# Soft-capped attention and a soft mixture of experts on one core: half tiles of the output started four products earlier, two evictions and a copy cut in two, and 14 more unused products

## The chip, the core and the metric

The kernel runs on one core of a Trainium2 chip. The core has five engines that run side by side, each with its own queue of instructions in order: TensorE (PE, matrix products, with loads of weights shown as PEld), VectorE (DVE), ScalarE (ACT), GpSimd (POOL) and SyncE (SP, which here only issues transfers). Products go to PSUM, a memory of eight banks, and from there ACT or DVE "evict" them, that is, copy them to SBUF, the large memory on the chip. Transfers between SBUF and HBM run on 16 DMA engines. The metric is the device time of one execution in microseconds.

## The reference

Sizes: 8 batches, 12 heads, 448 tokens, 64 columns a head; then 3584 rows of 768 columns, 8 experts with 4 slots each, hidden width 1024.

```python
scores = cap * tanh((q @ k.T) * scale / cap)
attn = exp(scores - max); attn = attn / (attn.sum(-1) + 1e-9)
x = (attn @ v)                       # as (3584, 768)
logits = x @ phi                     # (3584, 32)
d = softmax(logits, over the rows)
slot_input = d.T @ x                 # (32, 768)
for e in range(8):                   # 4 slots of each expert
    slot_out[e] = relu(slot_input[e] @ w1[e]) @ w2[e]
c = softmax(logits, over the slots)
out = c @ slot_out                   # (3584, 768), fp32
```

## The kernel before, in words

The program orders every engine's instructions by hand (`manual_schedule`); the framework adds the semaphores that the data and the banks need.

**Attention** fills the first 237 us. The 336 pairs of a key tile and two heads are worked off in 56 chunks of six (`CH`); chunk by chunk ACT takes the tanh and the exponential, DVE takes a part of the exponentials by a polynomial, and PE makes scores, the products with v, transposes and logits. What else is done in a chunk hangs in a table by chunk and slot (`at`, `run`). The table `FILL` (L805) puts unused products there: `fill(n)` (L661) issues n products of 57 columns whose result nobody reads. The row (7, 'a') of `FILL` applies to seven chunks: 7, 14, 21 and so on to 49.

**The weights** w1 and a part of w2 come to SBUF in this time; the rest of w2 is spilled to HBM as bf16 and fetched back by SP into `w2t` (L1057 to L1060) from 223 us on, when attention's buffers come free.

**The tail** starts with the last logits and slot sums (up to L1047). Then:

- `layer1` (L1074) multiplies the slots with w1, four experts at a time, and `relu` evicts; `h_transp` (L1091) turns the result. The order on PE is 72 products of layer 1, 8 of `h_transp(0)`, 48 of layer 1, 16 of layer 2, 8 of `h_transp(1)`, the rest of layer 2.
- `layer2` (L1105) multiplies with w2. Each call issues four products of 384 columns, for four experts, into one bank. The 64 products of half 0 (the first 384 output columns; L1161 to L1167) add up in `so_ps[0]`, the 64 of half 1 (L1170 on) in `so_ps[1]`.
- Between, L1168 copies the sum of half 0 to `so[0]` on ACT.
- While half 1 runs, 12 *half tiles* of the output are made from `so[0]` (L1173 to L1176). `half_tile` (L1142) issues one product of 384 columns into a bank of its own, has ACT or DVE scale it by `winv` into SBUF, and has SP store it (`store`, L1133). They come in pairs, one evicted by ACT and one by DVE.
- L1177 copies the sum of half 1 on DVE. The same 12 tiles then get their half 1, stored two at a time (L1190), and the last 16 tiles are made whole (L1192 to L1206).

PE, ACT, DVE and SP each work in the order in which these lines issue. A store waits for the eviction of what it writes.

Of the kernel before, what the change touches and what calls it, by code (L numbers as in the profile page):

```python
# [18 lines left out]
P = 128  # L19
# [18 lines left out]
def kernel(  # L38
# [18 lines left out]
    HD = D // 2  # L57
# [12 lines left out]
    pe, dve, act, pool, sp = nc.tensor, nc.vector, nc.scalar, nc.gpsimd, nc.sync  # L70
# [17 lines left out]
    winv = consts.tile([P, B // 2, NT], F32, name="winv")  # L88
# [655 lines left out]
    def et_tile(bb, c):  # L744
        return (ETl if bb == B // 2 - 1 else ET4[:, bb])[:, c, :, :].rearrange("p a q -> p (a q)")
# [50 lines left out]
    def at(j, slot, f, *a):  # L796
        if j < 0:
            j, slot = 0, "b"
        aux.setdefault((j, slot), []).append((f, a))
# [2 lines left out]

        busy(n, psV.tile([P, parts * P], F32, name="junk", tag="pv"))

    FILL = ((7, 'a', fill, 25), (6, 'c', spare, 7), (5, 'a', fill, 8),)  # L805
    PER = 2 * NQB * NT // CH
    assert PER == 7 and NQB == 3

# [15 lines left out]
    for b in range(B):  # L824
# [11 lines left out]
        if b == 0:  # L836
            at(j + 1, "d", spare, 14)
            at(j + 2, "d", spare, 5)
        for k, slot, f, n in FILL:
            if (b or k > 2) and j + k < NCH - 1:  # L840
# [110 lines left out]
    def bank(shape, dt=F32, name="bank"):  # L951
        n = turns.pop(0)
        if not turns:
            turns.extend((3, 2, 6, 0, 1))
        return big.tile(shape, dt, name=name, tag=f"b{n}")
# [147 lines left out]
    so_ps = []  # L1103

    def layer2(n0, half):  # L1105
        for n in range(n0, n0 + 4):
            i, ft, gg = blocks[n]
            pe.matmul(so_ps[half][32 * gg:32 * gg + NS, :],  # L1108
                      hpad[:, 4 * i + gg, ft, :],
                      w2_half(n, half),  # L1110
                      start=(n0 == 0), stop=(n0 == len(blocks) - 4))
# [6 lines left out]
    so = [t[:, 0:HD] for t in room]  # L1118
# [14 lines left out]
    def store(n, h0, h1, src, tokens=1):  # L1133
        bb, c = divmod(n, NT)
        width = (h1 - h0) * HD
        sp.dma_start(out=bass.AP(tensor=out.tensor,
                                 offset=(2 * bb * S + c) * D + h0 * HD,
                                 ap=[[NT * D, P], [1, tokens * D]] if width == D else
                                 [[NT * D, P], [D, tokens], [1, width]]),
                     in_=src)  # L1140

    def half_tile(n, half, home, eng):  # L1142

        bb, c = divmod(n, NT)
        if c == 0:
            obs[bb, half] = wts.tile([P, NT, HD], F32, name="obh", tag="w1", bufs=E)
        ob = obs[bb, half][:, c, :]
        pe.matmul(home, et_tile(bb, c), so[half], start=True, stop=True)  # L1148
        if eng == "dve":
            dve.tensor_scalar_mul(ob, home, winv[:, bb, c:c + 1])  # L1150
        else:
            act.mul(ob, home, winv[:, bb, c:c + 1])
        k = waiting.pop(half, n)
        if half and n + 1 < NH and c < NT - 1 and k == n:
            waiting[half] = n
            return
        store(k, half, half + 1, obs[bb, half][:, c - (n - k):c + 1, :], n - k + 1)

    NH = 12
    n2 = len(blocks)  # L1160
    for n0 in range(0, n2, 4):  # L1161
# [3 lines left out]
            for b in (B - 2, B - 1):  # L1165
                e_recips(b)
        layer2(n0, 0)  # L1167
    act.copy(so[0], so_ps[0])  # L1168
    done = 0
    for n0 in range(0, n2, 4):  # L1170
        layer2(n0, 1)

        if n0 % 8 == 4 and n0 > 4 and done < NH:  # L1173
            for eng in ("act", "dve"):
                half_tile(done, 0, bank([P, HD], name="op0"), eng)
                done += 1  # L1176
    dve.tensor_copy(so[1], so_ps[1])  # L1177
    mid.close()
# [3 lines left out]
    for n in range(B // 2 * NT):  # L1182
        bb, c = divmod(n, NT)
        if n == NH + 3:
            e_transp(B - 1)
        if n == NH + 5:
            e_transp(B - 2)
        op = fin.tile([P, 2, 512], F32, name="op", tag="op")
        if n < NH:
            half_tile(n, 1, op[:, 0, 0:HD], "act" if n % 2 else "dve")  # L1190
            continue
        for half in range(2):  # L1192
            pe.matmul(op[:, half, 0:HD], et_tile(bb, c), so[half],  # L1193
                      start=True, stop=True)

        if n == NH or c == 0 or full:
            ob, n1 = wts.tile([P, 2, 2, HD], F32, name="ob", tag="w1", bufs=E), n
        dst = ob[:, n - n1, :, :]
        if n % 2:
            dve.tensor_scalar_mul(dst, op[:, :, 0:HD], winv[:, bb, c:c + 1])  # L1200
        else:
            act.mul(dst, op[:, :, 0:HD], winv[:, bb, c:c + 1])  # L1202
        full = n > n1 or c == NT - 1
        if full:
            store(n1, 0, 2, ob[:, 0:n - n1 + 1, :, :].rearrange("p t a d -> p (t a d)"),
                  n - n1 + 1)  # L1206
# [35 lines left out]
```

## Time and profile before

| | us |
|---|---|
| median of three runs | 283.37 |
| the three runs | 282.81, 283.37, 283.69 |
| the profiled execution | 283.45 |
| its span in the trace | 281.7 |

The page of a profile gives each engine's busy time as a share of the span, then the span in 40 slices, the DMA queues, and the chain of work that ended last: from the last instruction back, at each step to whatever released it. "issue" in that chain is time in which an engine waited for nothing that the profile shows. A group's row gives line, engine, operation, the tile that is written and those that are read, the shapes, the number of instructions, their busy time, the mean of one in ns, and the idle time ahead of them with what ended it. A timeline's row gives start, length, engine, line and what was done; "x28" are 28 instructions that follow each other. The start of a product in the timeline is when it enters PE, and several overlap.

### The profile page before, as it was taken

What the parts mean: (1) busy time and instruction counts of PE and PEld (TensorE: products, weight loads), DVE (VectorE), ACT (ScalarE), POOL (GpSimd) and SP (SyncE); (2) the same over time, 40 slices, a digit from 0 to 9 for tenths busy, and PEclk for the clock granted to TensorE, in tenths of its full rate; (3) what the DMA queues carried; (4) which work ended last, traced back from release to release, by engine and by line L of the source; (5) the groups of instructions that cost most, each with busy time, mean ns of one, the idle gap of its engine ahead of it and who ended that gap; (6) DMA issues with size and microseconds to landing.
All of it is one profiled execution on the core that took longest, in us unless ns stands there. A gap on an engine that the chain in (4) does not pass through costs nothing.

```text
span 281.7 us, 10449 instructions
## 1 busy us (share of the span) xinstructions
PE 246.5 (88%) x4563; PEld 167.0 (59%) x4563; DVE 239.5 (85%) x474; ACT 249.1 (88%) x198; POOL 140.9 (50%) x198
## 2 busy tenths in 40 slices
PE   8897889998998999889998999899988999997720
PEld 7555556756665766566656675667565777642410
DVE  3479999999999999999999999999999996447840
ACT  3999999999999999999999999999999997236730
POOL 7885548662957285727673768285744120200000
PEclk9999999999999999999999999999999999999995
DMA  7999999999999999999999999999999589959997
GB/s 245 245 190 203 218 211 227 228 223 217 206 218 225 219 231 226 225 216 213 221 226 215 207 220 230 217 219 214 231 217 220 128 260 317 408 201 391 413 424 303
DMA packets 58332, 68.08 MB, mean 242 GB/s; under 512 B 4144, under 2 KB 54448, under 8 KB 58288
## 3 DMA queue, kind: packets, MB, share of 16 engines
q0 software_dynamic: 42448, 35.31, 79.7%
q1 hardware_dynamic: 15552, 31.89, 32.4%
q8 instruction: 35, 0.57, 0.7%
q10 hardware_dynamic: 288, 0.23, 0.3%
q14 instruction: 9, 0.07, 0.1%
HBM read 91.72 MB, written 19.27 MB: 394 GB/s over the span
## 4 chain that ended last, share of the span: by engine, by line
ACT 38%; PE 31%; DVE 20%; issue 5%; POOL 1%; DVEq 0%; ACTq 0%
ACT ex L374 16%; ACT ex L366 14%; PE pv L635 8%; ACT ex L362 7%; PE sc L349 4%; DVE xq L645 2%; DVE xp L615 2%; PE so_ps L1108 2%; PE hp L1080 2%; DVE xp L613 2%; DVE ex L616 2%; ACT ob L1202 2%; PE op L1193 1%; DVE xf L612 1%; PE op L1148 1%
## 5 line engine op out<-in xcount | busy, mean ns | idle before, releaser
L366 ACT ACTIVATE ex<-sc 128x1344 f16<-128x1344 f32 (+1 forms) x91 | 118.5, 1405 | 1.5 <-PE sc L349 1.5
L374 ACT ACTIVATE ex<-ex 128x1344 bf16<-128x1344 f16 (+5 forms) x58 | 110.2, 1911 | 0.1
L635 PE MATMUL pv<-vbd,ex 128*128 128x130 bf16 (+1 forms) x1610 | 95.0, 212 | 9.5 <-POOL vbd L289 3.9
L635 PEld LDWEIGHTS <-ex 128*128 128x128 bf16 (+1 forms) x1680 | 75.6, 101 | 38.1 <-issue 6.2
L289 POOL CAST vbd<-vraw 64x896 bf16<-64x896 f32 x46 | 47.3, 1027 | 60.2 <-PE pv L635 42.5
L349 PE MATMUL sc<-qT,kT 64*64 64x448 bf16 x672 | 66.4, 359 | 5.6 <-ACT ex L366 4.1
L349 PEld LDWEIGHTS <-kT 64*64 64x64 bf16 x672 | 22.4, 105 | 14.4 <-ACT ex L366 6.3
L645 DVE TENSOR_TENSOR xq<-pv,rec 128x448 bf16<-128x448 f32 x46 | 28.7, 625 | 1.6
L362 ACT ACTIVATE ex<-sc 128x2688 f16<-128x2688 f32 x11 | 28.1, 2552 | 0.1
L615 DVE TENSOR_TENSOR xp<-xp,xf 128x1344 f16<-128x1344 f16 (+2 forms) x34 | 27.5, 808 | 0.5
L616 DVE TENSOR_TENSOR ex<-ex,xp 128x1344 uint16<-128x1344 uint16 (+2 forms) x34 | 26.9, 791 | 0.2
L613 DVE TENSOR_TENSOR xp<-xf 128x1344 f16<-128x1344 uint16 (+2 forms) x34 | 26.9, 790 | 0.2
L116 POOL DMA_DIRECT2D w1b<-in_moe_w_dram x32 | 25.8, 808 | 0.0
L281 DVE COPY kT<-kps 128x896 bf16<-128x896 bf16 x23 | 14.2, 616 | 4.9 <-PE kps L276 2.8
L610 DVE TENSOR_SCALAR ex<-ex 128x1344 uint16<-128x1344 f16 (+2 forms) x34 | 17.0, 501 | 1.2 <-ACT ex L362 0.7
L614 DVE TENSOR_SCALAR xp<-xp 128x1344 f16<-128x1344 f16 (+2 forms) x34 | 17.0, 500 | 0.6
L612 DVE TENSOR_SCALAR xf<-ex 128x1344 uint16<-128x1344 uint16 (+2 forms) x34 | 17.2, 507 | 0.3
L185 POOL DMA_DIRECT2D qb<-in_q_dram x22 | 16.3, 739 | 1.5 <-PE qps L279 0.9
L297 POOL MEMSET vbd<- 64x1 bf16 x22 | 3.0, 138 | 27.7 <-PE pv L635 27.4
L617 DVE TENSOR_SCALAR ex<-ex 128x1344 uint16<-128x1344 uint16 (+2 forms) x34 | 16.5, 484 | 0.2
L185 POOL DMA_DIRECT2D kb<-in_k_dram x22 | 16.5, 748 | 0.0
L120 POOL DMA_DIRECT2D w2d<-in_moe_w_dram x21 | 16.1, 789 | 0.0
(124 smaller groups left out, 320.6 us busy)
## 6 DMA issues: line engine op xcount, KB each, us to landing
w1b<-in_moe_w_dram POOLq DMA_DIRECT2D x32, 384.0 KB, 9.6
vraw<-in_v_dram SPq DMA_DIRECT2D x44, 224.0 KB, 6.3
w2d<-in_moe_w_dram POOLq DMA_DIRECT2D x21, 384.0 KB, 9.7
w2t<-w2d SPq DMA_DIRECT2D x21, 384.0 KB, 6.5
out_dram<-ob SPq DMA_DIRECT2D x7, 768.0 KB, 6.8
qb<-in_q_dram POOLq DMA_DIRECT2D x22, 224.0 KB, 8.1
kb<-in_k_dram POOLq DMA_DIRECT2D x22, 224.0 KB, 7.7
w2b<-in_moe_w_dram POOLq DMA_DIRECT2D x11, 384.0 KB, 8.9
```

What stands on the lines that cost most here:

```text
L116: pool.dma_start(out=w1b[e][:, js, fs], in_=w1r[:, e, js, fs])
L185: pool.dma_start(out=t, in_=quad_ap(nm, Q))
L289: pool.tensor_copy(vbds[Q % 2][r, :, :, c0:c0 + DH], raw[r])
L349: ins = pe.matmul(sc[cs, u, 0:S], qkT["k", Q][r, c, cs], qkT["q", Q][r, :, cs], start=True, stop=True).ins
L362: apart["t", i - 1] = apart["t", i] = act.activation(exs[j].bitcast(F16), own["board"][:, :, 0:S], ACT.Tanh, scale=qk_scale / cap).ins
L366: ins = act.activation(exs[j][:, half * CS + u0:half * CS + u1, :].bitcast(F16), (own[0] if i == u0 == 0 else sc)[:, u0:u1, 0:S], ACT.Tanh ...
L374: act.activation(exs[j][:, u0:u1, :], exs[j][:, u0:u1, :].bitcast(F16), ACT.Exp, scale=cap)
L613: lambda: dve.tensor_tensor(p, s, s.bitcast(F16), op=ALU.mult),
L615: lambda: dve.tensor_tensor(p, p, s, op=ALU.mult),
L616: lambda: dve.tensor_tensor(y, y, p, op=ALU.add),
L635: pe.matmul(out_, exs[j][r, u, q0:q0 + (HP if tail else P)], v_, start=(c == 0 and g == gs[0] < NF), stop=(c == NT - 1), skip_group_check= ...
L645: dve.tensor_tensor(xq[Q][:, h, s0:s1, :], pv[:, 0:s1 - s0, 0:DH], rec.to_broadcast([P, s1 - s0, DH]), op=ALU.mult)
```

## The change

Four edits. The fills of row (7, 'a') have 27 products in place of 25, in seven chunks: 14 products in all. The half tiles of half 0 come after the layer-2 calls n0 = 8, 16, ..., 48 of half 1, and not after 12, 20, ..., 52: each pair stands one call, four products, earlier, and three calls follow the last pair in place of two. The first pair (n0 = 8) is evicted in two column halves, by ACT and then by DVE in the order of issue; the later pairs as before. The copy of the half-0 sum is cut likewise, 192 columns on ACT and 192 on DVE.

```diff
-    FILL = ((7, 'a', fill, 25), (6, 'c', spare, 7), (5, 'a', fill, 8),)
+    FILL = ((7, 'a', fill, 27), (6, 'c', spare, 7), (5, 'a', fill, 8),)
...
         pe.matmul(home, et_tile(bb, c), so[half], start=True, stop=True)
-        if eng == "dve":
-            dve.tensor_scalar_mul(ob, home, winv[:, bb, c:c + 1])
-        else:
-            act.mul(ob, home, winv[:, bb, c:c + 1])
+        cut = {"act": HD, "dve": 0, "both": HD // 2}[eng]
+        if cut:
+            act.mul(ob[:, 0:cut], home[:, 0:cut], winv[:, bb, c:c + 1])
+        if cut < HD:
+            dve.tensor_scalar_mul(ob[:, cut:HD], home[:, cut:HD], winv[:, bb, c:c + 1])
...
-    act.copy(so[0], so_ps[0])
+    act.copy(so[0][:, 0:HD // 2], so_ps[0][:, 0:HD // 2])
+    dve.tensor_copy(so[0][:, HD // 2:HD], so_ps[0][:, HD // 2:HD])
     done = 0
     for n0 in range(0, n2, 4):
         layer2(n0, 1)
 
-        if n0 % 8 == 4 and n0 > 4 and done < NH:
+        if n0 % 8 == 0 and n0 > 0 and done < NH:
             for eng in ("act", "dve"):
-                half_tile(done, 0, bank([P, HD], name="op0"), eng)
+                half_tile(done, 0, bank([P, HD], name="op0"), eng if n0 > 8 else "both")
                 done += 1
```

## The prediction

> **What bounds the kernel now.** I read the page first, then the stretches of the last 35 us, the chain of waits through them, the timeline for single instructions, and last the queues. The attention part, up to about 237 us, is shared out over PE, ACT and DVE; all of the change but the fills acts behind it. From the page:
>
> ```profile
> span 281.7 us, 10449 instructions
> PE 246.5 (88%) x4563; PEld 167.0 (59%) x4563; DVE 239.5 (85%) x474; ACT 249.1 (88%) x198; POOL 140.9 (50%) x198
> q8 instruction: 35, 0.57, 0.7%
> ```
>
> By stretch of the tail (stretch, its length, busy time of PE, PEld, DVE, ACT and POOL, clock, DMA share, GB/s):
>
> ```profile
> 246.00:248.00 2.00, 2.00 (x63) 1.32 (x55) 0.90 (x4) 0.47 (x1) 0.00 (x0) 1.00 1.05 414
> 250.00:251.00 1.00, 0.91 (x16) 0.44 (x17) 0.00 (x0) 0.00 (x0) 0.00 (x0) 1.00 0.08 31
> 254.00:258.00 4.00, 2.88 (x32) 0.86 (x27) 3.06 (x6) 2.15 (x4) 0.00 (x0) 1.00 1.05 393
> 259.00:279.00 20.00, 8.71 (x46) 4.08 (x45) 10.32 (x14) 9.06 (x12) 0.00 (x0) 0.90 1.03 417
> ```
>
> From 254 us to the end the transfers are full (share 1.03 to 1.05): the output's 11.0 MB (3584 x 768 fp32) is being written. From 250 to 251 next to nothing moves (0.08): the last weights are in, and no output is ready. So the end moves with the moment from which stores flow without a gap. What sets that moment stands in the chain of waits (start, length, what):
>
> ```profile
> 240.69 4.05 PE hp L1080 x72
> 244.74 0.29 PE hps L1097 x8
> 245.03 1.42 PE hp L1080 x48
> 246.46 0.65 PE so_ps L1108 x16
> 247.11 0.29 PE hps L1097 x8
> 247.40 2.22 PE so_ps L1108 x49
> 249.62 0.47 issue
> ...
> 255.74 0.52 DVE obh L1150
> 256.27 0.56 DVE so L1177
> 256.83 0.05 issue
> 256.88 0.35 PE op L1148
> ```
>
> It is PE back to back from 240.7, but for 0.47 us before product 66 of layer 2 (the second of half 1), which runs at 249.62 + 0.47 = 250.09. PE's waits in that stretch put it down to nothing:
>
> ```profile
> PE so_ps L1108 <- issue: 0.5, 1, 0.5
> ```
>
> It is the one pause of PE in the whole trace with no semaphore behind it. The instruction queue q8 has 35 packets for 9126 records of PE (4563 products, 4563 weight loads): one per about 130 products. One of them ran in the 1.1 us from 247.5, none between 244.0 and 247.5:
>
> ```profile
> q8 instruction: 1, 0.02, 5.0%
> ```
>
> 130 products before product 66 (65 + 8 + 48 + 8 of the chain) PE ended its first run of layer 1, at 244.7. I read: there PE stepped into a new block of instructions and asked for the one after it; the packet came late behind the weights' loads; at product 66 PE ran dry.
>
> **The change part by part.** Single instructions of the tail, by the timeline (start, length):
>
> ```profile
> 247.33 1.32 PE L1108 MATMUL so_ps<-w2b,hpad 128*32 128x384 bf16 x28
> 248.48 1.14 PE L1108 MATMUL so_ps<-w2t,hpad 128*32 128x384 bf16 x21
> 249.52 0.48 ACT L1168 CAST so<-so_ps 128x384 bf16<-128x384 f32 x1 [2.53 <-PE so_ps L1108]
> 250.85 0.50 PE L1148 MATMUL op<-so,ET 128*128 128x384 bf16 x2
> 251.22 0.58 ACT L1152 ACTIVATE obh<-op,winv 128x384 f32<-128x384 f32 x1 [1.23 <-PE op L1148]
> 251.46 0.62 DVE L1150 TENSOR_SCALAR obh<-op,winv 128x384 f32<-128x384 f32 x1 [2.25 <-PE op L1148]
> 255.63 0.51 PE L1108 MATMUL so_ps<-w2t,hpad 128*32 128x384 bf16 x8
> 256.27 0.55 DVE L1177 CAST so<-so_ps 128x384 bf16<-128x384 f32 x1
> ```
>
> and its groups (last numbers: busy, mean ns, idle before), with 768 columns beside 384 for the slopes:
>
> ```profile
> L1200 DVE TENSOR_SCALAR ob<-op,winv 128x768 f32<-128x768 f32 x8 | 8.0, 1016 | 2.7 <-PE op L1193 2.7
> L1150 DVE TENSOR_SCALAR obh<-op,winv 128x384 f32<-128x384 f32 x12 | 7.2, 617 | 4.2 <-PE op L1148 4.1
> L1202 ACT ACTIVATE ob<-op,winv 128x768 f32<-128x768 f32 x8 | 7.0, 898 | 2.9 <-PE op L1193 2.2 <-DMA out_dram<-obh 0.6
> L1152 ACT ACTIVATE obh<-op,winv 128x384 f32<-128x384 f32 x12 | 6.9, 580 | 4.6 <-PE op L1148 4.4
> L1108 PE MATMUL so_ps<-w2t,hpad 128*32 128x384 bf16 x84 | 5.0, 329 | 0.5 <-issue 0.5
> ```
>
> *The 14 products (2 in each of 7 fills).* With their weight loads they are 28 more PE instructions ahead of layer 1, so block edges fall 14 products earlier in all later work. Their own cost first:
>
> ```profile
> 63.46 0.83 PE L665 MATMUL pv<-ones 128*128 128x57 bf16 x25
> 65.98 0.49 PE L635 MATMUL pv<-vbd,ex 128*128 128x130 bf16 x5 [0.49 <-DVE ex L617]
> ```
>
> 25 take 0.83, the last about 0.19 of it, so 0.027 each: 0.37 for all 14 if nothing hides them. In the fill shown PE stands idle 0.49 two microseconds later for DVE, and the 0.05 that two more take ends there; of the other six, two wait for DVE in the same way and one for ACT, and three meet later waits. I take 0.05, between 0 and 0.37.
>
> *The pause.* One product lasts 0.33, so product 65 started at 249.62 - 0.33 = 249.29; 48 steps from 247.33 give 0.041 a product. Product 66 was due at 249.33 and ran at 250.09: 0.76 lost. After the change the edge lies before product 52, due at 249.33 - 14 x 0.041 = 248.76, still in half 0. The request moves 14 products of layer 1 ahead (4.05/72 = 0.056 each): 0.79. With the same time from request to use, PE goes on at R = 250.09 - 0.79 = 249.30, so 0.54 are lost in place of 0.76. That time is unknown for the new place: R can be 248.76 (in time) or 250.09 (the packet is served when it was served before). I take 249.30, the only row there is, and keep both ends.
>
> *The sum's copy split.* By the slopes, 192 columns less save ACT (898 - 580)/2 = 159 ns and DVE (1016 - 617)/2 = 200: halves of 0.32 and 0.35. Run together they would beat 0.48 by 0.13. But both read one bank, and the trace has no two engines reading one PSUM tile at a time. The tile that both do read:
>
> ```profile
> 4.76 0.47 ACT L238 COPY qT<-boot 64x384 bf16<-64x384 bf16 x1 [0.62 <-PE boot L236]
> 6.20 0.42 DVE L238 COPY kT<-boot 64x512 bf16<-64x512 bf16 x1 [0.27 <-PE boot L236]
> ```
>
> goes one after the other, and DVE's record there waits on ACT's counter beside PE's, though it uses nothing that ACT made. So I take the halves in turn: 0.32 + 0.05 (the handing over before 256.88) + 0.35 = 0.72, which is 0.24 more than now. The Trainium skill's page "PSUM — Partial Sum Buffer" (section "PSUM bank collisions raise a hardware error") says that two engines on one bank and quadrant at once are an error even when both only read, so a semaphore has to part them; by that rule the sum is the one taken here, and side by side it would be the third rival's; no run here shows the error.
>
> *Half tiles four products earlier.* From R: 13 products end half 0 (12 x 0.041 + 0.33 = 0.82), 0.05 to ACT, 0.72 of copies, 0.05 to PE: first half tile's product at T' = R + 1.64. PE itself would be there after 25 products, R + 1.03, and the 0.14 that passed between products and 250.85 before: R + 1.17. So PE, in order, now waits 0.47 for the sum, and the half-1 products queued behind wait with it. Before, T = 250.85 waited for nothing.
>
> *First two tiles by two engines.* Halves of 0.42 and 0.42, in turn: the first is whole at T' + 0.37 + 0.42 + 0.05 + 0.42 = T' + 1.26, its store follows 0.03 later at T' + 1.29. SP waits for both counters; only stores stand behind it. The stores:
>
> ```profile
> 251.83 0.34 SPq L1136 DMA_DIRECT2D out_dram<-obh  x1
> 258.02 0.38 SPq L1136 DMA_DIRECT2D out_dram<-obh  x1
> ```
>
> The first of half 0 left at T + 0.98, the first pair of half 1 at T + 7.17. Twelve stores of 0.197 MB at 393 GB/s take 6.0: they end at T' + 7.29.
>
> *What sets the end.* After the op products PE now has 52 products of half 1 left, not 48: 0.16 more, so half 1 ends at 256.30 where it ended at 256.14, both plus T' - T. DVE's copy of so[1] started at 256.27 because DVE was evicting; now PE is last and it starts 0.05 after PE: 0.08 later against T. The pair comes at T' + 7.25, level with the twelve stores: no gap opens, and the end moves with the pair. An earlier first tile alone moves nothing: it only opens a gap before the pair.
>
> Sum: R + 1.64 - 250.85 + 0.08 = R - 249.13 = +0.17 with R = 249.30; the fills add 0.05: +0.2. The profiled execution took 283.45 (1.75 around its span) and stands 0.08 above the median of 283.37; so 283.65 by its own time, 283.6 against the median.
>
> **The rivals.**
> 1. *The packet is not earlier* (slower). The request is earlier but waits behind the same loads; PE goes on at 250.09, with 14 products more still to do before the sum. Price 250.09 - 249.13 = +0.96, 284.4 with the fills; uncovered fills 284.7. It decides from R = 250.0. For it: the transfers are full up to 248 (1.05); against: PE's packet was served before those loads had drained.
> 2. *In time.* R = 248.76: -0.37, 283.05. For it: 14 products of layer 1 last longer than 14 of layer 2, and any wait in between helps too.
> 3. *Both engines read at once.* T' = R + 0.87 + 0.35 + 0.05 = R + 1.27, so the sum is R - 249.50: -0.2 at 249.30, 283.2; with an early packet -0.74, 282.7. Against it: the two copies from boot.
> 4. *The pause is not the packet's and the shift does nothing.* It stays before product 66. The sum is ready at 249.52 + 0.72 + 0.05 = 250.29, product 76 done by 250.09 + 11 x 0.041 + 0.14 = 250.68 = T': -0.17 + 0.08 + 0.05, 283.3. The Trainium skill's page "Runtime: NRT & Kernel Launch" (section "Instruction fetch mechanics") calls block edges mostly hidden and gives PE room for 2048 instructions, an argument for this rival; the 0.47 without a releaser is the row against it.
>
> **How the numbers follow.** A measurement of this kernel can tell about 0.3%, 0.85 us. Forecast 0.45 (within 0.37, slower 0.07, faster 0.01); first rival 0.25 (slower 0.20, within 0.05); second 0.13 (within 0.10, faster 0.03); third 0.09 (faster 0.04, within 0.05); fourth 0.08 (within 0.06, 0.01 each side). Together faster 0.09, within 0.63, slower 0.28. The range runs from the third rival's early end, 282.7, to the first's late end, 284.7. Both signs being likely, the forecast's own range is 283.2 to 284.2.
>
> **What would show it.** In the profile after: an "issue" pause of PE inside half 0, some 14 products before its end, shorter than 0.76; DVE's half of so[0] starting after ACT's half has ended, and the same in the first two tiles; the first store later against the first half tile's product than 0.98; DMA share above 1 from two microseconds behind that store without a dip at the first pair. I am wrong if the halves overlap, if the pause stays before product 66 or vanishes, or if the attention part ends elsewhere than at 237 by more than 0.4.

## The result and the profile after

| | before | after |
|---|---|---|
| median of 17 runs, us | 282.67 | 284.40 |
| range of the runs, us | 281.83 to 284.40 | 283.46 to 285.88 |
| profiled execution, us | 283.45 | 285.88 |
| its span, us | 281.7 | 284.1 |

The ratio is 1.0060, with a 95% interval of 1.0041 to 1.0079: the change makes the kernel slower, by 1.2 to 2.2 us. The forecast of 283.6 is 0.8 too low; 284.4 lies near the top of its range. The profiled execution after is the slowest of the 17, so of its 2.4 us of longer span some are scatter, and the traces have to be read from marks inside them.

From the page after:

```profile
PE 246.4 (87%) x4577; PEld 167.5 (59%) x4577; DVE 241.6 (85%) x476; ACT 249.2 (88%) x199; POOL 141.0 (50%) x198
q8 instruction: 36, 0.59, 0.8%
```

PE has 14 products and 14 weight loads more (4577 in place of 4563 each), and there is one instruction packet more: 36 in place of 35. The chain of waits through the tail (start, length, what):

```profile
241.59 4.05 PE hp L1080 x72
...
248.01 0.29 PE hps L1097 x8
248.30 1.57 PE so_ps L1108 x35
249.87 0.70 issue
250.57 0.84 PE so_ps L1108 x13
251.41 0.02 issue
251.43 0.33 ACT so L1169
251.76 0.02 issue
251.78 0.37 DVE so L1170
252.15 0.04 issue
252.19 0.49 PE op L1148 x2
...
257.69 0.56 DVE so L1179
```

Layer 1 starts 0.90 later than before (241.59 against 240.69). The pause has moved: 16 and 35 products of layer 2 come ahead of it, so it stands before product 52, and 14 products earlier than before, as worked out. DVE's half of the sum starts when ACT's has ended, and PE's next product starts 0.04 after DVE's half.

The first store of half 0 and the first pair of half 1, by SP's timeline (start, length):

```profile
253.45 0.34 SPq L1136 DMA_DIRECT2D out_dram<-obh  x1
259.44 0.38 SPq L1136 DMA_DIRECT2D out_dram<-obh  x1
```

Before, the pair left at 258.02. With the 0.90 of layer 1 taken off, it leaves 0.52 later now. But from the pair to the end of the span the kernel before takes 281.7 - 258.0 = 23.7 us, and the one after 284.1 - 259.4 = 24.7. This last 1.0 us is in no term of the prediction's sum. It lies where only transfers are at work. First the instruction queue between 252 and the end. Before, it has no row there at all. After:

```profile
q8 instruction: 1, 0.02, 0.2%
```

A narrower stretch, 266.0 to 267.6, holds that one packet: it runs amid the output. And the transfers in the 1.5 us that end 0.9 before each span's end, before and then after, as the transfers' own view counts them (a DMA row cuts the stretch into 40 slices; a digit is the busy share of the 16 engines in one slice, in tenths):

```profile
DMA packets 77, 0.19 MB, mean 125 GB/s; under 512 B 16, under 2 KB 16, under 8 KB 77
```

```profile
DMA  0200200200020020020020020000000000000000
DMA packets 10, 0.02 MB, mean 16 GB/s; under 512 B 2, under 2 KB 2, under 8 KB 10
```

Before, the engines end nearly together. After, ten packets follow each other one at a time over about a microsecond. I read this as one engine that is still writing when the other fifteen are done; the records don't name a packet's engine, so that this is the engine that took the instruction packet is an inference.

### The profile page after: what moved, and what is told of

It is laid out like the page before. It is cut to its first block, busy times and chain, and to the rows that moved or that the text cites. A ratio compares the mean times of both kernels' runs of the same rounds, so it can differ in the third digit from the quotient of the medians.

```text
span 284.1 us, 10477 instructions
## 1 busy us (share of the span) xinstructions
PE 246.4 (87%) x4577; PEld 167.5 (59%) x4577; DVE 241.6 (85%) x476; ACT 249.2 (88%) x199; POOL 141.0 (50%) x198
## 4 chain that ended last, share of the span: by engine, by line
PE 30%; ACT 28%; DVE 27%; issue 4%; DMA 4%; POOL 2%; DVEq 0%; SPq 0%; ACTq 0%
ACT ex L374 11%; ACT ex L366 11%; PE pv L635 10%; ACT ex L362 5%; PE sc L349 4%; DVE xq L645 3%; DVE xp L613 3%; DVE xp L615 3%; DVE ex L616 3%; DMA qraw<-in_q_dram 2%; DMA out_dram<-ob 2%; DVE qT L281 2%; DVE xf L612 2%; PE hp L1080 2%; DVE ex L610 2%
## 5 line engine op out<-in xcount | busy, mean ns | idle before, releaser
L366 ACT ACTIVATE ex<-sc 128x1344 f16<-128x1344 f32 (+1 forms) x91 | 117.0, 1375 | 2.3 <-PE sc L349 2.2
L374 ACT ACTIVATE ex<-ex 128x1344 bf16<-128x1344 f16 (+5 forms) x58 | 108.7, 1878 | 0.1
L616 DVE TENSOR_TENSOR ex<-ex,xp 128x1344 uint16<-128x1344 uint16 (+2 forms) x34 | 27.5, 809 | 0.2
```

Of the source, the lines that this page charges most:

```text
L366: ins = act.activation(exs[j][:, half * CS + u0:half * CS + u1, :].bitcast(F16), (own[0] if i == u0 == 0 else sc)[:, u0:u1, 0:S], ACT.Tanh ...
L374: act.activation(exs[j][:, u0:u1, :], exs[j][:, u0:u1, :].bitcast(F16), ACT.Exp, scale=cap)
L616: lambda: dve.tensor_tensor(y, y, p, op=ALU.add),
```

## The experiments

The theory that came out of the comparison: PE's program is fetched in blocks; the kernel before ends just short of a block's edge; 28 instructions more push it over, so a 36th packet of 16 KB (0.59 MB in 36 packets) runs while all engines write output, and the engine that carries it ends about 1 us after the others. The rivals: the cuts cost it, since the halves go in turn; or the fills cost PE time in attention. All ratios below are against the kernel before, run on the same chip, with 95% intervals.

**The fills alone.**

```diff
-    FILL = ((7, 'a', fill, 25), (6, 'c', spare, 7), (5, 'a', fill, 8),)
+    FILL = ((7, 'a', fill, 27), (6, 'c', spare, 7), (5, 'a', fill, 8),)
```

> The kernel before with the fills alone (27 for 25). Theory, the 36th packet: the 28 instructions push the end of PE's program over one more block edge, so one more instruction packet is fetched while the output is written, and the DMA engine that carries it is done 0.9 us after the others; the pause of PE moves to product 52, the sum of half 0 comes 0.2 later. Together 0.9 to 1.3 us slower than before, 36 packets on q8. Rival, the cut copies and evictions cost it: within 0.3 us of before. Rival, the fills cost PE time in attention: layer 1 starts up to 0.4 us later, the time grows by no more than that plus 0.2.

Measured: 1.0032 (1.0014 to 1.0051), 283.74 against 282.80. About half of the change's loss comes with the fills, none of it visible in attention: layer 1 starts at 240.41 in this trace, earlier than before. The page and the chain:

```profile
q8 instruction: 36, 0.59, 0.8%
```

```profile
247.12 2.77 PE so_ps L1108 x64
249.89 0.43 PE op L1148 x2
```

There are 36 packets; and in this execution there is no pause in layer 2 at all. The expected 0.2 us for the pause's new place were not there, and the time is still 0.9 us longer.

**The packet alone.** The same 14 products, but in the output's stage, where PE waits for evictions anyhow: behind the pause, and adding nothing to attention.

```diff
+        if n < NH + 14:
+            pe.matmul(op[:, 0, HD:HD + 57], ones, ones[:, 0:57], start=True, stop=True,
+                      skip_group_check=True)
         for half in range(2):
             pe.matmul(op[:, half, 0:HD], et_tile(bb, c), so[half],
```

> The kernel before with 14 unused products of 57 columns, one ahead of the products of each of the whole tiles 12 to 25, so behind the pause and in a stage where PE waits for evictions. Theory, the 36th packet: pause unchanged before product 66 (about 0.47 idle), 36 packets on q8 with one in the output's writing, 0.7 to 1.0 us slower. Every rival: no change, within 0.3 us.

Measured: 1.0041 (1.0025 to 1.0056), 283.78 against 282.80: 1.0 us for 14 products of 0.027 us in a stage that does not wait for PE. The page has the 36th packet, and the 1.5 us that end 0.9 before the span's end look as they do after the change:

```profile
q8 instruction: 36, 0.59, 0.8%
```

```profile
DMA packets 10, 0.02 MB, mean 16 GB/s; under 512 B 2, under 2 KB 2, under 8 KB 10
```

The expectation was wrong on one side point: the pause before product 66, in code that this edit does not touch, is missing from this trace. It comes and goes from one execution to the next.

**Fewer instructions, and the last packet among the stores.** If the packet's place counts and not its number, then taking 42 products out, so that packet 35 is asked for later, must cost as well.

```diff
-    FILL = ((7, 'a', fill, 25), (6, 'c', spare, 7), (5, 'a', fill, 8),)
+    FILL = ((7, 'a', fill, 19), (6, 'c', spare, 7), (5, 'a', fill, 8),)
```

> The kernel before with 42 unused products fewer (19 for 25), less work and nothing else. Theory, the packet in the output's writing: 35 packets, but the last of them, at 251.1 in the gap of the transfers before, is asked for some 42 products later and runs at 253 or later, among the stores; one engine then ends 0.9 to 1.0 after the median of the 16. The pause before product 66 cannot occur. Together +0.2 to +0.9 us. Rival, only the number of packets counts: 0 to 0.5 us faster. Rival, fills cost PE time: faster by up to 1 us.

Measured: 1.0042 (1.0023 to 1.0061), 284.02 against 282.62. With less work and no pause the kernel is slower by as much as with one packet more. The page has 35 packets; the stretch 253.8 to 255.0 of the transfers' view has the last of them, and the 1.5 us that end 0.9 before the span's end show the lone engine:

```profile
q8 instruction: 1, 0.02, 4.8%
```

```profile
DMA  0200200020020020020020020000000000000000
DMA packets 10, 0.02 MB, mean 16 GB/s; under 512 B 2, under 2 KB 2, under 8 KB 10
```

So it is the packet in the output's writing that costs, not the count. But the loss, 1.2 us by the ratio, is above the 0.2 to 0.9 expected, and this trace shows a second place where time goes. Just behind the packet the flow of stores breaks off: between 255 and 256 the transfers are busy for 0.45 of the time, where before they are full. SP takes 1.03 us to issue the store at 254.19, and 0.41 for the one ahead of it. First the stretch in the kernel before, then in this one, then SP's row:

```profile
255.00:256.00 1.00, 1.00 (x18) 0.23 (x10) 0.75 (x2) 0.71 (x2) 0.00 (x0) 1.00 1.05 393
```

```profile
255.00:256.00 1.00, 0.59 (x9) 0.12 (x8) 0.81 (x2) 0.58 (x1) 0.00 (x0) 1.00 0.45 164
```

```profile
254.19 1.03 SPq L1136 DMA_DIRECT2D out_dram<-obh  x1
```

**The change without the fills**, that is the early half tiles and both cuts.

```diff
-    FILL = ((7, 'a', fill, 27), (6, 'c', spare, 7), (5, 'a', fill, 8),)
+    FILL = ((7, 'a', fill, 25), (6, 'c', spare, 7), (5, 'a', fill, 8),)
```

> The changed kernel without the fills (25): early half tiles and both cuts stay. Theory, the 36th packet: 35 packets, the pause stays before product 66, and by the working of the fourth rival of the prediction the end moves by -0.1 us: within 0.3 us of before. Rival, the cuts cost it: about as slow as the changed kernel, 1.2 to 2.2 us above before.

Measured: 1.0015 (0.9997 to 1.0033), 282.99 against 282.80. The cuts are not most of the loss. Whether cuts and early tiles together cost some tenths of a microsecond or nothing isn't told.

**The early half tiles alone.**

```diff
-        if n0 % 8 == 4 and n0 > 4 and done < NH:
+        if n0 % 8 == 0 and n0 > 0 and done < NH:
```

> The kernel before with the half tiles four products earlier alone: no cuts, fills of 25. The pause stays before product 66; the first half tile's product comes 0.17 us earlier, half 1 ends 0.16 later against it: -0.1 us, within 0.3 us of before by every theory but one: if early stores alone were worth something, 0.3 us or more faster.

Measured: 1.0006 (0.9987 to 1.0025). As forecast, earlier stores are by themselves worth nothing that this interval can tell. The pause before product 66, which was expected to stay, is missing from this trace too.

**Both cuts alone**, at the old places (the change's cuts, with the pair behind n0 = 12 cut in place of that behind n0 = 8).

```diff
-        if n0 % 8 == 0 and n0 > 0 and done < NH:
+        if n0 % 8 == 4 and n0 > 4 and done < NH:
...
-                half_tile(done, 0, bank([P, HD], name="op0"), eng if n0 > 8 else "both")
+                half_tile(done, 0, bank([P, HD], name="op0"), eng if n0 > 12 else "both")
```

> The kernel before with both cuts alone: the sum's copy and the first pair of half tiles, at its old place behind n0 = 12; fills of 25. Theory, the halves run in turn on one bank: DVE starts its half when ACT's has ended; the sum is ready 0.25 later than an uncut one, which PE does not feel at n0 = 12; the first store leaves about 1.3 after the first half tile's product in place of 1.0; the end moves by +0.1 to +0.3. Rival, the halves overlap: first store 0.8 after that product, end unchanged or 0.1 earlier. 35 packets on q8 by both.

Measured: 1.0004 (0.9991 to 1.0017). That the halves go in turn stands in this trace's timeline too; DVE's wait names ACT:

```profile
249.10 0.32 ACT L1169 CAST so<-so_ps 128x192 bf16<-128x192 f32 x1 [2.53 <-PE so_ps L1108]
249.46 0.36 DVE L1170 CAST so<-so_ps 128x192 bf16<-128x192 f32 x1 [0.66 <-ACT so L1169]
```

**Both large effects at once, without the fills in attention**: the change with fills of 25 and the 14 products in the output's stage (the two edits shown above).

> The changed kernel with its 14 unused products moved: fills of 25, and one unused product ahead of each of the whole tiles 12 to 25. Nothing is added to attention and no edge ahead of the pause moves. Theory, the 36th packet plus the halves in turn: 36 packets, the last landing 1.2 to 1.8 us after the median engine's, and the sum of the two effects measured apart (0.15% and 0.41%): 0.4% to 0.7% slower than before, like the changed kernel. Rival, the fills' place in attention makes a good part of the loss: 0.3% or less.

Measured: 1.0053 (1.0034 to 1.0072). What the change costs (1.0060) comes back, within the intervals, with no fill added to attention. The two parts measured apart, 0.15% and 0.41%, add up to it, though 0.15% alone is not told from nothing. The trace has 36 packets and the same ten lone packets at the end.

**The change without the cuts**: early half tiles and fills of 27 (the first and the fifth edit).

> The changed kernel without both cuts: early half tiles and fills of 27. Theory: 36 packets, the last landing 1.2 to 1.8 us after the median engine's: 0.3% to 0.5% slower than before, 0.1% to 0.2% less than the changed kernel, since PE does not wait for the second half of the sum. Rival, the cuts cost nothing: 0.6% slower like the changed kernel. Rival, the cuts make most of the loss: 0.2% or less.

Measured: 1.0054 (1.0034 to 1.0074). That is just above the 0.3% to 0.5% expected: taking the cuts out of the change gains nothing that these intervals can tell, and the rival that they cost nothing isn't out. Here the pause is in the trace, before product 52, shorter than after, and PE waits for the whole sum on ACT:

```profile
247.33 1.57 PE so_ps L1108 x35
248.90 0.45 issue
249.35 0.84 PE so_ps L1108 x13
250.19 0.02 issue
250.21 0.49 ACT so L1168
```

**Two attempts at something faster**, with the edge a little behind product 66, so that the pause goes and the last packet still runs in the gap before the stores. First 21 products fewer.

```diff
-    FILL = ((7, 'a', fill, 25), (6, 'c', spare, 7), (5, 'a', fill, 8),)
+    FILL = ((7, 'a', fill, 22), (6, 'c', spare, 7), (5, 'a', fill, 8),)
```

> The kernel before with 21 unused products fewer (22 for 25). Theory: the block edge lies some 21 products behind product 66, where the half tiles' products give the request 0.6 us more, so the pause is short or gone; the last packet runs at 251.4 to 252.4, still ahead of the output's full flow. 0 to 0.6 us faster than before, the last landing within 0.6 of the median engine's. Rival, position does not matter: no change.

Measured: 1.0048 (1.0028 to 1.0068): a miss. The pause is gone, but the packet did not fall into the gap; it lies between 252.6 and 254.0, among the first stores:

```profile
q8 instruction: 1, 0.02, 3.9%
```

As with 42 products fewer, the flow of stores breaks off behind it: from 254 to 255 the transfers' share is 0.44.

Then 14 products fewer together with the early half tiles (the fifth edit and 23 for 25).

> The half tiles four products earlier, no cuts, and 14 unused products fewer (23 for 25). Theory: the edge lies at the second pair of half tiles; the pause is short or gone, the last packet runs around 251.5 and meets the first stores: between 0.6 us faster and 0.3 us slower than before. Rival, position does not matter: as the early half tiles alone, 0.1 us from before.

Measured: 1.0022 (1.0007 to 1.0037), 0.6 us slower and outside what was expected. Its last packet lies between 250.9 and 252.4, at the first stores. There it leaves no lone engine at the end but a gap at the start: SP's second store takes 1.38 us to issue, between 252 and 253 the transfers' share is 0.28 (1.07 with the early half tiles alone), and the first pair of half 1 leaves at 257.77 in place of 257.25. No version here beats the kernel before.

**All traces side by side**, in the order in which the last instruction packet starts. The first pair of half 1 is the first store that waits for the end of layer 2; from there to the end of the span only the output is left (us, one trace each):

| version | last packet starts | first pair leaves | from there to the end | time against before |
|---|---|---|---|---|
| early half tiles | 250.18 | 257.25 | 23.45 | 1.0006 |
| change without the fills | 250.60 | 257.34 | 23.66 | 1.0015 |
| both cuts | 251.03 | 257.85 | 23.70 | 1.0004 |
| early half tiles, fills of 23 | 251.04 | 257.77 | 23.64 | 1.0022 |
| before | 251.12 | 258.02 | 23.66 | 1 |
| fills of 22 | 252.83 | 258.18 | 24.02 | 1.0048 |
| fills of 19 | 253.92 | 257.80 | 25.02 | 1.0042 |
| fills of 27 | 263.98 | 256.99 | 24.51 | 1.0032 |
| early half tiles, fills of 27 | 264.99 | 257.99 | 24.68 | 1.0054 |
| the change | 266.55 | 259.44 | 24.66 | 1.0060 |
| change, 14 products moved | 267.89 | 256.87 | 24.86 | 1.0053 |
| 14 late products | 268.14 | 257.12 | 24.88 | 1.0041 |

In the five traces whose last packet starts before 252, the output takes 23.45 to 23.70 us from the first pair on; in the six whose packet starts at 253.9 or later, 24.51 to 25.02. Fills of 22, in between, lose part of their time in the gap at 254.

## Why the prediction was right or wrong

**Right in the range, wrong in the likeliest case.** "Within 0.3%" had 0.63; it came out at +0.60%, a case that had 0.28. That the time lies in the range is luck: its upper end, 284.7, was made of a packet served late ahead of the sum and of fills that attention doesn't hide, and what cost 1.0 us was in none of the cases.

**The step that failed** is the cost of the 14 products. The prediction counted their time on PE (0.05, between 0 and 0.37) and what they do to the pause. It did not follow the block edges on to the program's end: 28 instructions more also mean a packet more there. Its own rows held the hint, 35 packets with one edge 130 products from the next: from product 66 to the end PE has 63 products of layer 2, 24 and 32 for the tiles and 8 transposes, 127 in all, so by this count the next edge lay at the very end of the program. The term of 0.05 should have been about 1.0, as the fills alone (0.9 us) and the late products (1.0 us) measured it.

**The attention part of that term** was small, as worked out: with fills of 27 layer 1 started at 241.59, 240.41 and 240.62, with 25 between 240.05 and 240.69 in six traces, and with only 22 at 241.22. The 0.90 of the profiled execution after is scatter, not the fills, although by the prediction's own sign (more than 0.4) that trace alone would have counted against it.

**The pause.** That it belongs to a block of instructions is borne out: with 14 products more ahead it stands before product 52 (after; early half tiles with 27), with none more before product 66. The size is another matter. In the trace after, product 51 started at 249.87 - 0.33 = 249.54, so product 52 was due at 249.58 and ran at 250.57: 0.99 lost where 0.54 were worked out. But it is not a fixed cost: it is missing from the traces of the fills alone, the late products, the early half tiles and the change with its products moved. One row before was taken for a constant.

The instruction packet that precedes the edge tells these traces apart. Before, it ran from 247.65 to 248.53, 0.8 us ahead of the 249.33 at which product 66 was due. With the early half tiles alone, whose instructions are the same up to there, it ran from 246.78 to 247.66, 1.6 ahead, and PE did not stop. In the five traces with a pause the packet ended 0.3 to 0.8 us ahead of the product that was due, and PE went on 1.25 to 1.58 us after the packet's end; in the four with this edge and no pause it ended 1.3 to 2.1 ahead.

**From the pause to the first pair** the working holds. R = 250.57 less the 0.90 is 249.67, and R - 249.13 gives +0.54; the pair moved by +0.52. The first half tile's product came at R + 1.62 (1.64 worked out), its store 1.26 later (1.29).

**The copies and evictions in turn** were right. The Trainium skill's page "PSUM — Partial Sum Buffer" (section "PSUM bank collisions raise a hardware error") asks for a semaphore between two engines that use one bank, and the traces agree: after, as with both cuts alone, DVE's read of the bank waits for ACT's. What they cost in the end can't be told from nothing (1.0004 with an upper end of 1.0017).

**The rivals.** The first had the right sign and nearly the right price, 284.4, by another mechanism: its packet, served as late as before, was not what cost 1.0 us. The second, no pause, was seen in single executions, and did not decide. The third is out: the halves go in turn. The fourth is out as far as the shift goes, since the pause did move by 14 products. The Trainium skill's page "Runtime: NRT & Kernel Launch" (section "Instruction fetch mechanics") calls the crossing of a block's edge mostly hidden, and here it was not: 0.41% for one packet at a bad place.

**What stays open**: why the packet ahead of the pause starts early in one execution and late in another; why SP's next store is held up behind a packet among the first stores; and how the rest of 0.60 - 0.41 = 0.19% (the two intervals overlap) splits over the cuts, the early tiles and the pause's place: cuts and early tiles alone each lie within their interval of nothing, and the pause's place was not measured alone.

## What to carry to other kernels

Count instructions to the end of each engine's queue, not only work: an edit that adds idle-time products can cost a packet of instructions, and what matters is what the DMA engines do when that packet runs. In this output stage, with the transfers full (share 1.03 to 1.06), one packet beside the stores came out at the end, or as a gap in their flow. Before a change is costed by moving an edge, follow every edge behind it as well, and take a pause of unknown cause from more than one execution.

## What the runs showed that was not expected

One packet of 16 KB, among 11.0 MB of output, made the kernel 0.41% (0.25% to 0.56%) slower. Taking 42 products away cost as much (0.42%) as adding 14. And a pause of 0.43 to 0.70 us (idle time of PE) that looks like a property of the program is there in some executions of the same instructions and absent in others.
